# Reordering four small things in a TensorE-bound kernel: square, gate, weights' sums and a check line

## The chip, the cores and the metric

The kernel runs on one core of a Trainium2 chip. The metric is the device time of one execution in microseconds (us), the median of several runs. Every comparison below is between runs in the same state; all runs of this case were in the fast state, and every kernel named here gave a correct result.

## The reference

Two blocks follow one another. The first is a gated linear attention with a complex decay per step (4 batches, 8 heads, 768 steps, head size 48); the second multiplies its output (3072 x 384) by a weight matrix, applies h * cos(h), and multiplies by a second weight matrix.

```python
# attention, for every batch and head, step t
scale = min(mag, 0.999) / (mag + 1e-6)          # mag = |a_re + i a_im|
new_re = ar * S_re - ai * S_im                  # ar, ai: a_re, a_im times scale
new_im = ar * S_im + ai * S_re
S_re, S_im = new_re + outer(k[t], v[t]), new_im
y[t] = q[t] @ S_re
# ... x = y laid out as (3072, 384) ...
h = x @ w_in                                    # (3072, 2048)
g = h * np.cos(h)
out = g @ w_out                                 # (3072, 384)
```

## The kernel before

The kernel works through 24 chunks of 128 steps in 12 groups of two. In each group ("n" below) TensorE computes one group's scores and states, the "hp" phase (x times w_in, eight tiles of 128 x 512 in PSUM, 12 matmul records each), and the products with w_out. The scheduler weaves the steps of neighbouring groups together; each engine then runs its own list in a fixed order, and `behind(a, b)` only says "a comes after b in that order", without any new semaphore.

These are the parts that the change touches. The eight hp tiles share three PSUM buffers (two of tag "m", one "acc"):

```python
def mm1(g, jp):                       # one hp tile and its gate
    ps = pm.tile([C, 2, G * C], F32, tag="acc" if third else "m", name="hp",
                 bufs=1 if third else 2)
    # ... 2 x 3 matmuls into ps ...
    special(out=gate, in_=ps, func=AF.Sin, scale=1.0 / in_scale, bias=half_pi_b)   # ScalarE: cos
    vector.tensor_tensor(out=gate, in0=ps, in1=gate, op=ALU.mult)                  # VectorE: h * cos
    scalar.activation(out=junk, in_=ps, func=AF.Square, scale=1.0 / in_scale,      # ScalarE: only for
                         accum_out=wide[:, ds(g * (NJ // 2) + jp, 1)])             #   the check
```

```python
def f_transpose(g, i, n, name):       # kT and qT of the next group; VectorE, then DMAs
    # ...
    vector.transpose(out=tr, in_=X[g][name[0] + "s"][:, ds(i * H, n * H)].rearrange(...))
    nc.sync.dma_start(out=moved..., in_=tr)
    # kT: four dma_starts; qT: one
    nc.sync.dma_start(out=X[g][name][:, :, ds(i * H, n * H)], in_=moved.rearrange("q c x j -> c q x j"))

# differences of quarters of w_out (the code's "t1, t2, t4"), for a product scheme with fewer matmuls
for t, a, b in (t1, b12, b11), (t2, b22, t1), (t4, b21, t2):
    yield lambda t=t, a=a, b=b, j=j: vector.tensor_tensor(
        out=t[:, ds(j, 2)], in0=a[:, ds(j, 2)], in1=b[:, ds(j, 2)], op=ALU.subtract)
```

At the end a "check line" of 224 single words is written to memory in two pieces (`low`, `even`), read back as one row, and reduced to one flag (`bad`). The flag says whether the fast path was allowed for these inputs.

```python
nc.sync.dma_start(out=line_d[0:D2], in_=low.rearrange("p o -> (p o)"))       # 96 single words
nc.sync.dma_start(out=line_d[D2:D2 + C], in_=even.rearrange("p o -> (p o)")) # 128 single words
nc.sync.dma_start(out=line, in_=line_d.unsqueeze(0))
nc.vector.tensor_reduce(out=bad[:, 0:1], in_=line, axis=AX.X, op=ALU.min)
```

Of the kernel before, what the change touches and what calls it, by code (L numbers as in the profile page):

```python
# [18 lines left out]
ALU = mybir.AluOpType  # L19
AX = mybir.AxisListType  # L20
# [466 lines left out]
def fast_path(ctx, tc, q, k, v, a_re, a_im, moe_w_in, moe_w_out, out, least, odd, wide):  # L487
# [6 lines left out]
    nc = tc.nc  # L494
    B, H, S, D = q.shape
    DM, DF = moe_w_in.shape
    C = 128
    NCH = S // C
    G = 2
    N = B * NCH  # L500
    NG = N // G
    D2 = 2 * D
    HH = H // 2
# [3 lines left out]
    NJ = DF // C  # L507
# [34 lines left out]
    X = [dict() for _ in range(NG)]  # L542
    Y = [dict() for _ in range(N)]
# [32 lines left out]
    causal = constant(causal_np * np.float32(0.25), "causal")  # L576
# [63 lines left out]
    in_scale = 2.0 if moe_w_in.dtype != F32 else 1.0  # L640
    out_scale = 2.0 if moe_w_out.dtype != F32 else 1.0

    tail = {}

    def chain(ins, engine="scalar"):
# [5 lines left out]
    def behind(ins, other):  # L651
        tc.add_manual_dep(ins.ins, other.ins.name, mybir.DependencyInfo(
            mybir.DependencyClass.NoSync, mybir.DependencyReason.DATA))
# [5 lines left out]
    class Ordered:  # L659
# [7 lines left out]
        def __getattr__(self, op):  # L667
            def call(**kw):
                ins = getattr(self.engine, op)(**kw)  # L669
                if Ordered.by_hand:  # L670
                    chain(ins, self.name)
                elif self.name in Ordered.mark:
                    behind(ins, Ordered.mark[self.name])
            return call

    vector, scalar = Ordered(nc.vector, "vector"), Ordered(nc.scalar, "scalar")
# [176 lines left out]
    def f_transpose(g, i, n, name):  # L853


        if i == 0:
            X[g][name] = ft.tile([D2, G * H, Q4, 32] if name == "kT" else [D2, Q4, G * H, 32], F32,
                                 tag=name, name=name, bufs=1)
        tr = ft.tile([C, NB, n * H, 32], F32, tag="tr", name="tr")
        vector.transpose(out=tr, in_=X[g][name[0] + "s"][:, ds(i * H, n * H)].rearrange(  # L860
            "p x a d -> p x (a d)").rearrange("p x (r b) -> p b x r", b=NB))
        moved = rows_d.tile([Q4, D2, n * H, 32], F32, tag="moved", name="moved", bufs=3)
        nc.sync.dma_start(out=moved.rearrange("q (r b) x j -> (q r) b x j", b=NB), in_=tr)
        if name == "kT":
            for q4 in range(Q4):
                nc.sync.dma_start(out=X[g][name][:, ds(i * H, n * H), q4], in_=moved[q4])
        else:
            nc.sync.dma_start(out=X[g][name][:, :, ds(i * H, n * H)],
                              in_=moved.rearrange("q c x j -> c q x j"))
# [18 lines left out]
    def f_scores(n, hh):  # L888
        y = Y[n]
        if hh == 0:  # L890
            y["atm"] = ft.tile([C, H, C], F32, tag="atm", name="atm")
        ps = pa.tile([C, HH, C], F32, tag="a", name="sc")
        for h in range(HH):
            head = hh * HH + h
            matmul(ps[:, h], lhsT=X[n // G]["kT"][:, n % G * H + head],
                   rhs=queries(n, head), start=True, stop=True)
        vector.tensor_tensor(out=y["atm"][:, ts(hh, HH)], in0=ps,
                                in1=causal.unsqueeze(1).to_broadcast([C, HH, C]), op=ALU.mult)

    def f_out(n):  # L900
        y, (g, i) = Y[n], divmod(n, G)
# [58 lines left out]
    def f_xt(g):  # L960

        moved = rows_d.tile([HH, 2, D, G * C], F32, tag="x", name="x")
        for side in range(2):
            nc.sync.dma_start(
                out=moved[:, side].rearrange("p d t -> d p t"),
                in_=X[g]["yT"][ds(side * 64, D)].rearrange("d p g t -> d p (g t)"))
        xt = X[g]["xT"] = msb.tile([C, ND, G, C], F32, tag="xT", name="xT")
        nc.sync.dma_start(
            out=xt.rearrange("p c g t -> p c (g t)"),
            in_=moved.rearrange("p s d t -> (p s d) t").rearrange("(c r) t -> r c t", r=C))  # L970

    def mm1(g, jp):
        x = X[g]
        third = len(x.setdefault("gate", {})) % 3 == 2
        ps = pm.tile([C, 2, G * C], F32, tag="acc" if third else "m", name="hp",
                     bufs=1 if third else 2)
        for ji in range(2):
            for dc in range(ND):
                matmul(ps[:, ji], lhsT=w_in[:, jp, dc, ts(ji, C)],
                       rhs=x["xT"][:, dc].rearrange("p g t -> p (g t)"),  # L980
                       start=(dc == 0), stop=(dc == ND - 1))
        gate = msb.tile([C, 2, G * C], F32, tag="gate", name="gate", bufs=8)
        junk = msb.tile([C, 2, G * C], BF16, tag="junk", name="junk", bufs=1)
        special(out=gate, in_=ps, func=AF.Sin, scale=1.0 / in_scale, bias=half_pi_b)
        vector.tensor_tensor(out=gate, in0=ps, in1=gate, op=ALU.mult)
        scalar.activation(out=junk, in_=ps, func=AF.Square, scale=1.0 / in_scale,
                             accum_out=wide[:, ds(g * (NJ // 2) + jp, 1)])
        x["gate"][jp] = gate

    def mm2(g, i, j0, nj):  # L990
# [20 lines left out]
    def quarters():  # L1011

        for name in "s1", "s2", "a22":
            right[name] = stage["pool"].tile([C, HJ, E2], F32, name="t_" + name)
        t1, t2, t4 = (right[name] for name in ("s1", "s2", "a22"))
        for j in range(0, HJ, 2):
            for t, a, b in (t1, b12, b11), (t2, b22, t1), (t4, b21, t2):
                yield lambda t=t, a=a, b=b, j=j: vector.tensor_tensor(
                    out=t[:, ds(j, 2)], in0=a[:, ds(j, 2)], in1=b[:, ds(j, 2)], op=ALU.subtract)

    def last_quarter():

# [25 lines left out]
    def seventh(g, p, part):  # L1048


        x, name = X[g], SEVEN[p]
        if p == 0 and part == 0:
            x["sum"] = pm.tile([C, E2], F32, tag="acc", name="sum", bufs=1)
            x["ot"] = [msb.tile([C, DM], F32, tag="ot", name="ot") for _ in range(G)]

        alone = g == NG - 1 and p == 6
        summed = p in (0, 3, 5, 6) and not alone
        if not summed and part == 0:
            x["op"] = pm.tile([C, E2], F32, tag="m", name="op", bufs=2)
        ps = x["sum"] if summed else x["op"]  # L1060
        for j in range(part * HJ // 2, (part + 1) * HJ // 2):
            matmul(ps, lhsT=left(g, name, j), rhs=right[name][:, j],
                   start=(j == 0 and (p == 0 or not summed)),
                   stop=(j == HJ - 1), skip_group_check=summed)
        if part == 0:
            return
        c11, c12, c21, c22 = (x["ot"][i][:, ts(half, E2)] for i in range(2) for half in range(2))
        if p in (0, 2, 5) or p == 6 and not alone:
            scalar.mul(out={0: c11, 2: c21, 5: c22, 6: c12}[p], in_=ps, mul=scale)
        if g == NG - 1 and p == 5:  # L1070
            scalar.mul(out=c12, in_=ps, mul=scale)
        if p in (1, 3, 4, 5) or alone:
            part_ = {1: c11, 3: c21, 4: c21, 5: c22, 6: c12}[p]
            vector.scalar_tensor_tensor(out=part_, in0=x["op"] if p == 5 else ps, scalar=scale,
                                        in1=part_, op0=ALU.mult, op1=ALU.add)
        row = g * G * C
        if g == NG - 1 and p == 1:
            nc.sync.dma_start(out=out[ds(row, C), 0:E2], in_=c11)
        elif p == 5:
            nc.sync.dma_start(out=out[ds(row + C, C), :], in_=x["ot"][1])  # L1080
        elif p == 6:
            nc.sync.dma_start(out=out[ds(row, C), ds(alone * E2, DM - alone * E2)],
                              in_=c12 if alone else x["ot"][0])
# [144 lines left out]
              (mixes(n, 0, 2), 0.9, 1.0), (guarded(n - 1, per) if n > 3 else [], 0.1, 0.9))  # L1228
    weave((mixes(NG - 1, 2, 4), 0.0, 0.1), (products(NG - 1, 0, 7), 0.0, 1.0))
    assert not guards  # L1230
@with_exitstack
def kernel(ctx, tc, q, k, v, a_re, a_im, moe_w_in, moe_w_out, out):

# [7 lines left out]
    NG, NJ = q.shape[0] * q.shape[2] // C // 2, moe_w_out.shape[0] // C  # L1241
    odd = keep.tile([C, moe_w_in.shape[0] // C * 4 + NJ + NG + 1], F32, name="odd")
    wide = keep.tile([C, NG * NJ // 2], F32, name="wide")
    fast_path(tc, q, k, v, a_re, a_im, moe_w_in, moe_w_out, out, least, odd, wide)
    low = keep.tile([D2, 1], F32, name="low")
    nc.vector.tensor_reduce(out=low, in_=least, axis=AX.X, op=ALU.min)
    even = keep.tile([C, 1], F32, name="even")
# [6 lines left out]
    scratch = ctx.enter_context(tc.tile_pool(name="scratch", bufs=1,  # L1254
                                             space=bass.MemoryType.DRAM))
    line_d = scratch.tile([D2 + C], F32, name="line_d")
    nc.sync.dma_start(out=line_d[0:D2], in_=low.rearrange("p o -> (p o)"))
    nc.sync.dma_start(out=line_d[D2:D2 + C], in_=even.rearrange("p o -> (p o)"))
    line = keep.tile([1, D2 + C], F32, name="line")
    nc.sync.dma_start(out=line, in_=line_d.unsqueeze(0))  # L1260
    bad = keep.tile([1, 2], F32, name="bad")
    nc.vector.tensor_reduce(out=bad[:, 0:1], in_=line, axis=AX.X, op=ALU.min)
    flag = keep.tile([1, 1], I32, name="flag")
    nc.vector.tensor_scalar(out=flag, in0=bad[:, 0:1], scalar1=0.5, scalar2=None, op0=ALU.is_lt)
    taken = nc.values_load(flag[0:1, 0:1], min_val=0, max_val=1,
# [33 lines left out]
```

## Time and profile before

| | kernel before |
|---|---|
| time, median of 3 runs (range) | 703.81 us (701.42 to 705.78) |
| span of the profiled run | 700.8 us |
| mean granted clock of TensorE | 0.981 |
| TensorE, VectorE, ScalarE busy | 94%, 69%, 55% |
| largest waits of TensorE that the change aims at | hp for the square 10.9 us in 9; hp for xT 2.6; phs for VectorE's tan 2.5; sum for ot 1.1 |
| length of an hp phase, with the wait / without | 22.13 us / 20.88 us |

TensorE is the bound, so the time can only be found in its gaps. In the list of waits a line reads: engine and tile that waited, what released it, total us, number of waits, the longest. In a timeline a line reads: start us, duration, engine, source line, operation, output from inputs, shapes, number of instructions in the stretch, and in brackets the idle time before it with what ended that. Tile names repeat: "junk" is the square's output, "gate" with "hp" among its inputs is VectorE's product, "tr" a transposition. The lines themselves are shown in the prediction.

### The profile page before, as it was taken

To read this page: it belongs to the slowest core of one execution; us is meant where nothing else is said; L and a number is where in the kernel's file an instruction comes from. 1 tells how busy PE (TensorE), PEld (TensorE's weight loads), DVE (VectorE), ACT (ScalarE), POOL (GpSimd) and SP (SyncE) were. 2 spreads that over 40 slices of the span, in tenths; PEclk is the share of its full clock that TensorE was granted. 3 is DMA by queue.
4 is the path that set the end of the run, shared out by engine and by line. 5 is a ranking of instruction groups with operands and counts; after the bars stand their busy time and mean duration, and the time that the engine had idled before them with its cause. 6 is when DMAs were issued, how large, how long until landed. Compare 5 with 4: busy or idle time off the path is not lost.

```text
span 700.8 us, 10680 instructions
## 1 busy us (share of the span) xinstructions
PE 659.7 (94%) x4060; PEld 579.7 (83%) x4060; DVE 480.9 (69%) x782; ACT 386.8 (55%) x710; POOL 26.1 (4%) x45
## 2 busy tenths in 40 slices
PE   5788898999999999999999999999999999899995
PEld 5686676886799899899899899899899899799894
DVE  4889899546767777776777777776777768752241
ACT  5867775374374376376376376376376376342330
POOL 1012100000000000000000000000000000000000
PEclk9978999999999999999999999999999999999999
DMA  9778707805636547656746747647746644453000
GB/s 256 154 226 253 189 21 144 207 1 124 169 68 124 168 116 162 171 119 151 189 113 137 204 112 154 180 118 160 182 112 156 183 114 73 131 135 91 23 1 29
DMA packets 232953, 94.96 MB, mean 136 GB/s; under 512 B 208814, under 2 KB 221361, under 8 KB 232892
## 3 DMA queue, kind: packets, MB, share of 16 engines
q1 hardware_dynamic: 226396, 68.68, 43.8%
q0 software_dynamic: 5632, 25.17, 10.7%
q8 instruction: 34, 0.56, 0.3%
q10 hardware_dynamic: 864, 0.33, 0.2%
q14 instruction: 27, 0.22, 0.1%
HBM read 69.35 MB, written 24.81 MB: 134 GB/s over the span
## 4 chain that ended last, share of the span: by engine, by line
PE 66%; DVE 16%; DMA 7%; ACT 7%; issue 2%; SPq 0%; POOL 0%; DVEq 0%; POOLq 0%
PE hp L679 24%; PE op L679 14%; PE sum L679 9%; PE sc L679 5%; DVE tr L669 5%; PE yp L679 5%; PE sp L679 3%; DVE qs L669 2%; PE phs L679 2%; DMA raw<-in_moe_w_out_dram 2%; PE lgs L679 2%; DVE w_out L669 2%; DVE ks L669 1%; ACT lg L698 1%; DMA xT<-x 1%
## 5 line engine op out<-in xcount | busy, mean ns | idle before, releaser
L679 PE MATMUL hp<-xT,w_in 128*128 128x256 f32 x1152 | 257.8, 384 | 14.1 <-ACT junk L669 10.9
L679 PEld LDWEIGHTS hp<-xT,w_in 128*128 128x128 f32 x1152 | 220.6, 192 | 49.7 <-ACT junk L669 14.5
L669 DVE TENSOR_TENSOR gate<-hp,gate 128x512 f32<-128x512 f32 x96 | 65.9, 686 | 88.7 <-ACT gate L698 87.8
L669 ACT ACTIVATE junk<-hp 128x512 bf16<-128x512 f32 x96 | 57.2, 596 | 94.1 <-DVE gate L669 94.1
L679 PE MATMUL op<-w_out,gate 128*128 128x192 f32 (+1 forms) x448 | 103.0, 379 | 0.6 <-DVE w_out L669 0.6
L679 PEld LDWEIGHTS op<-w_out,gate 128*128 128x128 f32 x448 | 76.5, 192 | 21.3 <-issue 3.2
L698 ACT ACTIVATE gate<-hp,half_pi_b 128x512 f32<-128x512 f32 x96 | 65.4, 684 | 44.6 <-PE hp L679 44.6
L679 PE MATMUL sum<-t_s,s 128*128 128x192 f32 x320 | 55.4, 326 | 1.1 <-DVE ot L669 1.1
L679 PEld LDWEIGHTS sum<-t_s,s 128*128 128x128 f32 x320 | 52.5, 190 | 1.4 <-DVE ot L669 1.4
L679 PEld LDWEIGHTS sc<-qT,kT 96*128 96x128 f32 x384 | 47.9, 192 | 2.7 <-ACT qT L669 1.2
L679 PE MATMUL sc<-qT,kT 96*128 96x128 f32 x384 | 49.2, 275 | 0.9 <-ACT qT L669 0.9
L669 ACT ACTIVATE ot<-sum 128x192 f32<-128x192 f32 x30 | 9.5, 320 | 59.7 <-PE sum L679 59.7
L669 DVE SCALAR_TENSOR_TENSOR ot<-op,ot 128x192 f32<-128x192 f32 x31 | 11.0, 356 | 39.9 <-ACT ot L669 26.3
L669 DVE TENSOR_TENSOR atm<-sc,causal 128x512 f32<-128x512 f32 x48 | 32.8, 684 | 6.0 <-PE sc L679 6.0
L694 ACT ACT_TABLE_LOAD x26 | 33.4, 1283 | 4.0 <-issue 3.6
L679 PE MATMUL yp<-atm,v 128*48 128x128 f32 x352 | 33.6, 277 | 0.6 <-DVE atm L669 0.6
L679 PEld LDWEIGHTS sp<-v,ks 128*96 128x96 f32 x320 | 29.7, 165 | 1.8 <-issue 1.0
L679 PE MATMUL yp<-qT,state 96*48 96x128 f32 x304 | 29.6, 272 | 0.0
L679 PE MATMUL sp<-v,ks 128*96 128x48 f32 x320 | 29.6, 245 | 0.0
L679 PE MATMUL sum<-w_out,gate 128*128 128x192 f32 x160 | 29.6, 329 | 0.0
L679 PE MATMUL op<-t_a,gate 128*128 128x192 f32 x160 | 29.0, 332 | 0.0
L669 ACT COPY yT<-yp 48x512 f32<-48x512 f32 x44 | 25.4, 577 | 6.5 <-PE yp L679 5.8
(123 smaller groups left out, 935.9 us busy)
## 6 DMA issues: line engine op xcount, KB each, us to landing
moved<-tr SPq DMA_DIRECT2D x20, 768.0 KB
raw<-in_moe_w_in_dram POOLq DMA_DIRECT2D x16, 768.0 KB, 6.1
raw<-in_moe_w_out_dram POOLq DMA_DIRECT2D x16, 768.0 KB, 5.0
kT<-moved SPq DMA_DIRECT2D x40, 192.0 KB
qT<-moved SPq DMA_DIRECT2D x10, 768.0 KB
k<-in_k_dram SPq DMA_DIRECT2D x24, 192.0 KB
q<-in_q_dram SPq DMA_DIRECT2D x24, 192.0 KB
v<-in_v_dram SPq DMA_DIRECT2D x24, 192.0 KB
```

The source lines that it names most:

```text
L669: ins = getattr(self.engine, op)(**kw)
L679: chain(nc.tensor.matmul(out, **kw), "tensor")
L694: chain(nc.scalar.preload_act_table_set(table))
L698: chain(nc.scalar.activation(func=func, **kw))
```

## The change

There are four parts. (1) In the hp phase ScalarE's square of a tile comes before VectorE's product, and VectorE runs the first tile's product between the two transpositions of the next group rather than behind both. (2) The weights' sums move from the crowded start of VectorE's list to a place behind the masks of the third group's scores. (3) The small transfer `low` goes behind the last transfer of xT. (4) The reduction `bad` goes behind the last output's addition. No matmul is added or removed. The diff, cut to its core (the omitted lines only hand instruction objects around):

```diff
@@ f_transpose
-        vector.transpose(out=tr, ...)
+        turn = vector.transpose(out=tr, ...)
+        if name == "qT" and "gated" in X[g - 1]:
+            behind(turn, X[g - 1]["gated"])
@@ f_scores
-        vector.tensor_tensor(out=y["atm"][:, ts(hh, HH)], in0=ps, ...)
+        y["masked"] = vector.tensor_tensor(out=y["atm"][:, ts(hh, HH)], in0=ps, ...)
@@ mm1
-        vector.tensor_tensor(out=gate, in0=ps, in1=gate, op=ALU.mult)
         scalar.activation(out=junk, in_=ps, func=AF.Square, ...)
+        gated = vector.tensor_tensor(out=gate, in0=ps, in1=gate, op=ALU.mult)
+        x.setdefault("gated", gated)
@@ the weights' sums
-                yield lambda t=t, a=a, b=b, j=j: vector.tensor_tensor(
-                    out=t[:, ds(j, 2)], in0=a[:, ds(j, 2)], in1=b[:, ds(j, 2)], op=ALU.subtract)
+                yield lambda t=t, a=a, b=b, j=j: behind(vector.tensor_tensor(
+                    out=t[:, ds(j, 2)], in0=a[:, ds(j, 2)], in1=b[:, ds(j, 2)],
+                    op=ALU.subtract), Y[PLAIN * G]["masked"])
@@ the check line
-    nc.sync.dma_start(out=line_d[0:D2], in_=low.rearrange("p o -> (p o)"))
+    behind(nc.sync.dma_start(out=line_d[0:D2], in_=low.rearrange("p o -> (p o)")), late["x"])
...
-    nc.vector.tensor_reduce(out=bad[:, 0:1], in_=line, axis=AX.X, op=ALU.min)
+    behind(nc.vector.tensor_reduce(out=bad[:, 0:1], in_=line, axis=AX.X, op=ALU.min), late["out"])
```

## The prediction

> **What bounds the kernel now.** I read the page first (busy time per engine), then the waits of TensorE, then the timeline of one steady group, the last groups and the end, and last the busy time by stretch for the start. The work is done in 12 groups of two chunks; each has a phase of eight "hp" tiles (x times the first weight matrix; 96 matmul records a group, 12 a tile), which ScalarE and VectorE turn into gates.
>
> The page's first part, busy us, share of the span and instructions; then TensorE's waits: total us, times, longest:
>
> ```profile
> PE 659.7 (94%) x4060; PEld 579.7 (83%) x4060; DVE 480.9 (69%) x782; ACT 386.8 (55%) x710; POOL 26.1 (4%) x45
> ...
> PE hp L679 <- ACT junk L669: 10.9, 9, 3.1
> PE phs L679 <- ACT tan L698: 4.0, 2, 2.7
> ...
> PE hp L679 <- DMA xT<-x: 2.6, 1, 2.6
> PE phs L679 <- DVE tan L669: 2.5, 2, 2.0
> PE sum L679 <- DVE ot L669: 1.1, 1, 1.1
> ```
>
> TensorE is the bound: 660 of 701 us. The change takes no matmul away and, as the comparison of the two programs' orders shows, leaves the order of TensorE and GpSimd exactly as it was. So all it can win is TensorE's idle time (some 41 us, of which the start and the end cannot be had) and time at a reduced clock. The largest named wait is the first: hp waits for the ScalarE square ("junk"). The timeline of a steady group (start us, duration, engine):
>
> ```profile
> 232.43 7.93 PE L679 MATMUL hp<-xT,w_in 128*128 128x256 f32 x36
> ...
> 235.22 0.69 ACT L698 ACTIVATE gate<-hp,half_pi_b 128x512 f32<-128x512 f32 x1 [2.24 <-PE hp L679]
> ...
> 235.53 2.24 DVE L669 STREAM_TRANSPOSE tr<-ks 128x1536 f32<-128x1536 f32 x1
> ...
> 237.75 2.24 DVE L669 STREAM_TRANSPOSE tr<-qs 128x1536 f32<-128x1536 f32 x1
> ...
> 239.92 0.64 DVE L669 TENSOR_TENSOR gate<-hp,gate 128x512 f32<-128x512 f32 x1
> 240.60 0.60 ACT L669 ACTIVATE junk<-hp 128x512 bf16<-128x512 f32 x1 [4.69 <-DVE gate L669]
> ...
> 241.34 3.94 PE L679 MATMUL hp<-xT,w_in 128*128 128x256 f32 x17 [0.98 <-ACT junk L669]
> ```
>
> There are three PSUM buffers for hp. Three tiles are 36 matmuls, so the fourth (due at about 240.0) needs the first one back. The first tile was ready at 235; its sine ran at once; but the VectorE product stood behind two transpositions of 2.24 us, and the square behind the product. ScalarE sat idle 4.69 us for it.
>
> [...] sine, product and square of a tile never overlap, and the square waited for the product 79 times (94.1 us in ScalarE's waits). [...]
>
> **Part 1: square before product, first gate between the transpositions.** The sum of a tile's own three steps stays (0.69 + 0.60, or 0.73 with the accumulator's read, + 0.69, about 2.1 us). But the square now follows the sine at once, 235.9 to 236.6, and the product needs only VectorE: behind the first transposition, 237.8 to 238.5. That gives the buffer back at 238.5 in place of 241.2, 1.5 us before the fourth tile is due. The second transposition then runs 238.5 to 240.7, the second product to 241.4; the fifth tile is due a tile (2.57 us) after the fourth, at 242.5. So the wait should vanish. Its worth is not 0.98 (ends of matmuls are modelled) but the length of the whole phase: 232.43 to 241.34 + 13.22 (the chain's remaining 60) = 254.56, so 22.13 us, against 20.88 us for the 96 of the last group, which has no wait. The same sums give 1.16 us in the third group and 1.25 in each of seven more: **9.9 us**.
>
> **Part 2: the start, where the weights are converted.** Busy us by stretch (TensorE, weight loads, VectorE, ScalarE, GpSimd), granted clock, DMA:
>
> ```profile
> 40.00:60.00 20.00, 16.67 (x73) 14.20 (x71) 16.56 (x24) 16.49 (x22) 2.41 (x3) 0.74 0.72 227
> 60.00:80.00 20.00, 15.42 (x49) 11.21 (x50) 16.33 (x23) 15.83 (x28) 3.83 (x5) 0.83 0.90 246
> 80.00:100.00 20.00, 19.37 (x91) 13.86 (x90) 19.96 (x31) 15.66 (x27) 0.72 (x1) 1.00 0.24 60
> 100.00:120.00 20.00, 17.99 (x149) 14.04 (x148) 19.18 (x32) 11.60 (x20) 0.00 (x0) 0.94 0.51 107
> ```
>
> The wait of 3.1 us (58.8 to 61.9) goes, since the new ScalarE order is sine, square, sine, square ahead of the conversions' casts; the exponentials and the phase matmul (waited 2.7 us) come some 4 us earlier. But from 80 to 117 VectorE is full and TensorE waits for it (0.6 us for the last w_out, 2.0 us for tan at 116.9). VectorE's work is fixed, so what counts is VectorE: the idle time it recovers between 60 and 80 (3.7 us, of which I give 2, as the products still wait for squares), and the weights' sums that leave this stretch (before 116.9: six sums of 0.55 us, 3.2 us on the clock). That would be about 5; TensorE itself can gain only 0.6 + 2.0 plus what the earlier conversions bring, and the last w_out fetches, freed by VectorE, come later in the new order. I take **4.5 us**, the softest term. The sums land at 150 to 170, where VectorE is about 55% busy (10.62 and 11.24 of 20 us); they put at most 1.1 us before the log that TensorE needs at 160.0, which was ready at 156.96. No cost.
>
> **Part 3: the check line's first half behind the last xT.** The eleventh group's hp starts late:
>
> ```profile
> 593.73 0.31 SPq L1257 DMA_DIRECT2D line_d<-low  x1
> ...
> 594.15 0.38 SPq L968 DMA_DIRECT2D xT<-x  x1
> ...
> 603.65 8.69 PE L679 MATMUL hp<-xT,w_in 128*128 128x256 f32 x39 [2.63 <-DMA xT<-x]
> ```
>
> From issue to use is 9.5 us here; in an earlier group 6.9 us (382.9 to 389.9) were enough without a wait. In the timeline, a transfer of this kind ("even", 0.5 KB of single words) took 6.4 us from its issue at 677.7 until the next one could be issued at 684.1. "low" now goes behind xT: I take 2.3 of the 2.6 us.
>
> **Part 4: the check line's reduction last.** Now it blocks VectorE for its DMA:
>
> ```profile
> 687.24 0.37 DVE L1262 TENSOR_REDUCE bad<-line 1x1 f32<-1x224 f32 x1 [7.50 <-DMA line<-line_d]
> ...
> 687.75 0.36 DVE L669 SCALAR_TENSOR_TENSOR ot<-sum,ot 128x192 f32<-128x192 f32 x1
> ...
> 688.17 2.87 PE L679 MATMUL sum<-t_s,s 128*128 128x192 f32 x16 [1.08 <-DVE ot L669]
> ```
>
> The "ot" sum had its operand at about 684.3; without the block TensorE loses nothing: **1.2 us**. What comes after the last matmul (693.6 to 700.8) I leave: the last output still goes out after it.
>
> Sum: 9.9 + 4.5 + 2.3 + 1.2 = 17.9. From it I take 1.6 for new small waits: 703.8 - 17.9 + 1.6 = **687.5 us**, 2.3% less.
>
> **Rivals.** (a) A transfer takes the wait's place. The second transposition ends 0.7 us later and TensorE reaches the next scores 1.25 us earlier. In one group qT's transfer is issued at 245.87, DMA traffic ends at about 251, the scores start at 254.4: 3 us of room, 1 left. The tightest is 561.70, 567, 569.55: 2.4 us, some 0.4 left. If it runs out, up to 1 us a group returns, and the time is about 694. (b) The start gives nothing, because VectorE stays full until the last w_out and its new order puts conversions behind the gates, so the log of the next group slips: about 692. Against it: 3.2 us of sums do leave. (c) The start gives more: without the stall of 3.1 us the clock stays up and TensorE's 60 to 80 shrinks as well; about 683. (d) VectorE becomes the bound in the hp phase: no, a pair of tiles costs it two products and four sums (2 x 0.69 + 4 x 0.42 = 3.1 us) in 5.1 us.
>
> **Range and chances.** Parts 1 and 4 are read from gaps that the new order removes by construction, 11.1 us together, with qT as the risk; they alone give 692.7, 1.6% less. Whether 2% (689.7) is passed hangs on parts 2 and 3. All good gives 682, only part 1 with some loss 694. Faster by over 2%: 0.66; within: 0.33; slower: 0.01, as nothing is added.
>
> **What would show it.** Part 1: in the waits no "hp <- junk", nor a new "hp <- gate"; every steady hp phase 20.9 us; one product between the transpositions. Part 2: hp's fourth tile of the first group starts near 59, clock above 0.8 in 40 to 80, the phase matmul at 116.9 comes at about 112. Part 3: no wait for xT. Part 4: no idle TensorE between the last products, "bad" without a wait. I am wrong if scores wait for kT or qT, or if VectorE reaches the end of the w_out conversions no earlier than 98 us.

## The result, and the profile after

| | before | after |
|---|---|---|
| time, median of 4 runs each, same rounds (range) | 703.16 us (701.42 to 705.78) | 684.19 us (683.15 to 686.43) |
| ratio, 95% interval | | 0.9731 (0.9691 to 0.9772): faster |
| span of the profiled run, mean clock | 700.8 us, 0.981 | 681.9 us, 0.987 |

A ratio here is the mean time of one kernel's fast runs over the mean time of the other's in the same rounds, so it is not quite the ratio of the two medians. Where a gain in us is given from a ratio below, it is (1 - ratio) times the median of the kernel before in that set of runs.

The page of the changed kernel, first part (busy us, share of the span, instructions):

```profile
PE 653.7 (96%) x4060; PEld 577.7 (85%) x4060; DVE 480.3 (70%) x782; ACT 382.5 (56%) x710; POOL 27.3 (4%) x45
```

The instruction counts of TensorE, VectorE and ScalarE are those of before: only order has changed. The waits of TensorE in the changed kernel:

```profile
PE phs L683 <- ACT tan L702: 4.2, 2, 2.8
...
PE op L683 <- DVE w_out L672: 2.3, 3, 1.1
PE phs L683 <- DVE tan L672: 2.1, 4, 0.8
PE sc L683 <- DMA qT<-moved: 1.3, 2, 0.9
```

Three of the four entries that the change aimed at, hp for junk, hp for the xT transfer and sum for VectorE's ot, are no longer in the list. The fourth, phs for VectorE's tan, fell only from 2.5 to 2.1 us in all; its longest piece fell from 2.0 to 0.8. Two things are new or larger: TensorE waits 2.3 us for converted weights (0.6 before), and 1.3 us for the qT transfer, which was no wait before. The timeline of a steady hp phase after the change, one group after the one the prediction shows:

```profile
277.80 13.54 PE L683 MATMUL hp<-xT,w_in 128*128 128x256 f32 x62
...
280.90 2.25 DVE L672 STREAM_TRANSPOSE tr<-ks 128x1536 f32<-128x1536 f32 x1
281.18 0.59 ACT L672 ACTIVATE junk<-hp 128x512 bf16<-128x512 f32 x1
...
283.12 0.69 DVE L672 TENSOR_TENSOR gate<-hp,gate 128x512 f32<-128x512 f32 x1
...
283.72 2.25 DVE L672 STREAM_TRANSPOSE tr<-qs 128x1536 f32<-128x1536 f32 x1
```

The square runs beside the first transposition, the product comes between the two, and the row of hp matmuls runs on past the 36th without a break (62 in one stretch, ended by other work woven in). Taking the first and last hp matmul of every group, groups 2 to 12 all last 20.88 us.

The busy time by stretch in the start (columns as in the prediction), two of the four stretches:

```profile
60.00:80.00 20.00, 16.84 (x70) 12.92 (x69) 19.35 (x29) 17.16 (x30) 3.62 (x5) 1.00 0.86 227
...
100.00:120.00 20.00, 18.77 (x129) 13.15 (x126) 17.63 (x26) 10.19 (x17) 0.00 (x0) 1.00 0.70 140
```

VectorE now works 19.35 of 20 us between 60 and 80 (16.33 before), with a granted clock of 1.00 (0.83 before); between 100 and 120 it has room again. The second group's hp phase starts at 121.2 against 127.1.

The eleventh group's transfer of xT (the last but one), its hp phase, and the small transfer, which now goes behind the twelfth group's xT, the last:

```profile
579.63 0.38 SPq L974 DMA_DIRECT2D xT<-x  x1
...
587.41 2.97 PE L683 MATMUL hp<-xT,w_in 128*128 128x256 f32 x13
...
628.26 0.48 SPq L1272 DMA_DIRECT2D line_d<-low  x1
```

From issue to use is 7.8 us instead of 9.5, with no wait in brackets. The end:

```profile
669.82 2.76 PE L683 MATMUL sum<-t_s,s 128*128 128x192 f32 x16
...
672.42 2.76 PE L683 MATMUL op<-w_out,s 128*128 128x192 f32 x16
...
673.26 0.36 DVE L1278 TENSOR_REDUCE bad<-line 1x1 f32<-1x224 f32 x1
```

The reduction no longer waits, and the products follow one another without idle time.

Where the 18.9 us of span went, from the starts of the hp phases in the two traces (the first starts 0.2 us apart): group 2 starts 5.9 us earlier (127.1 against 121.2), group 10 13.4 us earlier (547.6 against 534.2), group 11, where the xT wait went, 16.2 us (603.6 against 587.4), group 12 17.1 us, and the end is 18.9 us earlier. Between the starts of groups 2 and 10 seven phases became 8.7 us shorter in all, but the start of group 10 gained only 7.5 of that; the new waits for qT lie in this stretch.

### The profile page after: what moved, and what is told of

The parts are those of the page before. It is cut to its first block, busy times and chain, and to the rows that moved or that the text cites. A ratio compares the mean times of both kernels' runs of the same rounds, so it can differ in the third digit from the quotient of the medians.

```text
span 681.9 us, 10685 instructions
## 1 busy us (share of the span) xinstructions
PE 653.7 (96%) x4060; PEld 577.7 (85%) x4060; DVE 480.3 (70%) x782; ACT 382.5 (56%) x710; POOL 27.3 (4%) x45
## 3 DMA queue, kind: packets, MB, share of 16 engines
q1 hardware_dynamic: 226396, 68.68, 44.6%
q0 software_dynamic: 5632, 25.17, 11.0%
## 4 chain that ended last, share of the span: by engine, by line
PE 84%; DMA 5%; DVE 5%; ACT 4%; issue 1%; DVEq 0%; ACTq 0%
PE hp L683 31%; PE op L683 17%; PE sum L683 15%; PE sc L683 6%; PE yp L683 5%; PE sp L683 3%; PE lgs L683 2%; DMA raw<-in_moe_w_out_dram 2%; PE phs L683 2%; DMA qT<-moved 2%; DVE w_in L672 1%; ACT raw L672 1%; DVE w_out L672 1%; PE yr L683 1%; DMA im<-in_a_im_dram 1%
## 5 line engine op out<-in xcount | busy, mean ns | idle before, releaser
L683 PE MATMUL hp<-xT,w_in 128*128 128x256 f32 x1152 | 253.6, 382 | 0.6 <-ACT xT L672 0.6
L683 PE MATMUL op<-w_out,gate 128*128 128x192 f32 (+1 forms) x448 | 101.6, 375 | 2.3 <-DVE w_out L672 2.3
L672 ACT CAST tan<-phs 128x384 int32<-128x384 f32 x24 | 11.5, 479 | 30.8 <-PE phs L683 30.6
```

The source lines that it names most:

```text
L672: ins = getattr(self.engine, op)(**kw)
L683: chain(nc.tensor.matmul(out, **kw), "tensor")
```

## The experiments

Runs that stand in one set ran on the same chip beside the same runs of the kernel before. Each kernel was timed in five rounds.

### First set: one part alone, on the kernel before

The kernel before had a median of 703.63 us here (27 runs).

**e1_swap_only**: only the order of square and product.

```diff
-        vector.tensor_tensor(out=gate, in0=ps, in1=gate, op=ALU.mult)
         scalar.activation(out=junk, in_=ps, func=AF.Square, ...)
+        vector.tensor_tensor(out=gate, in0=ps, in1=gate, op=ALU.mult)
```

> Edit: the kernel before, with only the square put ahead of the product. Theory A (the release of the first PSUM tile is the limit, and it still stands behind both transpositions): product of the first tile at 239.98 to 240.65 in the old clock, the fourth tile due at 240.0, so a wait of some 0.7 us remains in 8 groups, now 'hp <- gate' in place of 'hp <- junk'; steady hp phase about 21.5 us (before 22.13, after 20.88), 0.55 x 8 = 4.5 us gained. In the start the wait of 3.1 us at 58.8 vanishes and the second group's hp phase starts 2 to 3 us earlier than 127.1. Time 7 us less than before. Rival B (the swap is the whole cure, the order of the transpositions is decoration): steady phase 20.9 us, time 13 us or more less.

Measured: 694.24 us, ratio 0.9871 (0.985 to 0.9892), 9.1 us less. The timeline of a steady phase in e1_swap_only:

```profile
284.04 2.25 DVE L669 STREAM_TRANSPOSE tr<-ks 128x1536 f32<-128x1536 f32 x1
...
286.26 2.27 DVE L669 STREAM_TRANSPOSE tr<-qs 128x1536 f32<-128x1536 f32 x1
...
288.44 1.26 DVE L669 TENSOR_TENSOR gate<-hp,gate 128x512 f32<-128x512 f32 x2
...
289.15 2.21 PE L680 MATMUL hp<-xT,w_in 128*128 128x256 f32 x9 [0.28 <-DVE gate L669]
```

The square is out of the way, but the product still stands behind both transpositions and the buffer comes back at about 289.1, just too late: a short wait for "gate" takes the place of the one for "junk" (2.6 us in 9 over the kernel). The phase lasts 21.43 us: 0.70 less than before, 0.55 more than without a wait. Over the eight phases that is 5.6 of the 9.9 us. The rest comes from the start, where the second group's hp begins at 123.5 instead of 127.1, 3.6 us earlier where 2 to 3 were expected.

**e2_turn_only**: only the product between the transpositions; the square stays behind the product.

```diff
-        vector.transpose(out=tr, ...)
+        turn = vector.transpose(out=tr, ...)
+        if name == "qT" and "gated" in X[g - 1]:
+            behind(turn, X[g - 1]["gated"])
...
-        vector.tensor_tensor(out=gate, in0=ps, in1=gate, op=ALU.mult)
+        gated = vector.tensor_tensor(out=gate, in0=ps, in1=gate, op=ALU.mult)
+        x.setdefault("gated", gated)
```

> Edit: the kernel before, with only the first product put between the two transpositions (the square stays behind the product). Theory A: product 237.8 to 238.5, square to 239.2, its accumulator's read to 239.4, and the tile is due at 240.0: no wait, though the old order of square and product stays. Steady hp phase 20.9 us, 9.9 us gained, start unchanged (wait of 3.1 us at 58.8 stays, second hp phase at 127). Time 10 us less than before. Rival B (swap needed): a wait of 0.5 us or more stays in each group, less than 6 us gained. Rival C (qT's transfer is late): scores wait for qT in two or three groups, 2 us of the 10 lost.

Measured: 693.54 us, ratio 0.9869 (0.9839 to 0.9899), 9.2 us less. The timeline of a steady phase in e2_turn_only:

```profile
284.13 2.25 DVE L669 STREAM_TRANSPOSE tr<-ks 128x1536 f32<-128x1536 f32 x1
...
286.34 0.70 DVE L669 TENSOR_TENSOR gate<-hp,gate 128x512 f32<-128x512 f32 x1
...
286.94 2.27 DVE L669 STREAM_TRANSPOSE tr<-qs 128x1536 f32<-128x1536 f32 x1
287.07 0.60 ACT L669 ACTIVATE junk<-hp 128x512 bf16<-128x512 f32 x1 [2.56 <-DVE gate L669]
```

The square still waits 2.56 us for the product, and it does not matter: it ends at 287.7. The phase began at 281.04, and 36 matmuls take some 7.8 us of it, so the fourth tile is due only at about 288.9. All steady phases last 20.88 us. In the steady groups the turn alone is enough; the swap adds nothing there. The stall of 3.1 us at the start stays, as no instruction moved there. The second hp phase came at 124.9 all the same, not at 127 as expected; the paragraph behind e8 says why.

**e3_sums_only**: only the weights' sums behind the third group's masks.

```diff
-                yield lambda t=t, a=a, b=b, j=j: vector.tensor_tensor(
-                    out=t[:, ds(j, 2)], in0=a[:, ds(j, 2)], in1=b[:, ds(j, 2)], op=ALU.subtract)
+                yield lambda t=t, a=a, b=b, j=j: behind(vector.tensor_tensor(
+                    out=t[:, ds(j, 2)], in0=a[:, ds(j, 2)], in1=b[:, ds(j, 2)],
+                    op=ALU.subtract), Y[PLAIN * G]["masked"])
```

> Edit: the kernel before, with only the twelve sums of the second weight matrix put behind the third group's masks. Theory A (VectorE bounds 80 to 117 us): the phase matmul that waited at 116.9 comes 2.0 to 3.2 us earlier without a wait, and as TensorE does not idle there its clock stays up (the 24 op matmuls that took 9.53 us take about 8.0), so the second hp phase starts 3 to 4.5 us earlier than 127.1; the 3.1 us wait at 58.8 stays; steady phases as before. Time 3 to 4 us less. Rival D (the sums were beside other work and cost nothing): within 1 us of before.

Measured: 701.94 us, ratio 0.9976 (0.9967 to 0.9985), 1.7 us less. The expectation was too high. The mechanism is there: the wait of phs for VectorE's tan fell from 2.5 us (longest 2.0) to 1.3 (longest 0.8). The second hp phase did start 3.9 us earlier in this profile (123.2), as expected, but 1.6 us of that is the faster run of 24 matmuls that e2 shows without moving the sums (granted clock 1.00 from 100 to 140 in both, 0.94 and 0.97 in before), and the profiled run was the fastest of the 22 (700.31 us).

**e4_line_only**: both check-line moves, parts 3 and 4.

```diff
-    nc.sync.dma_start(out=line_d[0:D2], in_=low.rearrange("p o -> (p o)"))
+    behind(nc.sync.dma_start(out=line_d[0:D2], in_=low.rearrange("p o -> (p o)")), late["x"])
...
-    nc.vector.tensor_reduce(out=bad[:, 0:1], in_=line, axis=AX.X, op=ALU.min)
+    behind(nc.vector.tensor_reduce(out=bad[:, 0:1], in_=line, axis=AX.X, op=ALU.min), late["out"])
```

> Edit: the kernel before, with only the two moves of the check line (low behind the last xT, the reduction behind the last output's sum). Theory A: no wait of 2.6 us for xT in the eleventh group, no 1.1 us wait of sum for ot at 688: 3.8 us less. Rival E (xT is late for another reason, such as the traffic before it): the wait for xT stays at 2 us or more and only 1.2 us is gained.

Measured: 697.5 us, ratio 0.9914 (0.9894 to 0.9934), 6.1 us less, against 3.8 expected. The waits for xT and for ot are gone and nothing else moved. The surplus had to be taken apart; e11 and e12 below do that.

### Second set: the changed kernel with one part taken back

The kernel before had a median of 703.4 us here (9 runs).

**e5_no_swap**: the changed kernel with the product before the square again.

```diff
+        gated = vector.tensor_tensor(out=gate, in0=ps, in1=gate, op=ALU.mult)
         scalar.activation(out=junk, in_=ps, func=AF.Square, ...)
-        gated = vector.tensor_tensor(out=gate, in0=ps, in1=gate, op=ALU.mult)
```

> Edit: the changed kernel with the square put back behind the product; all else of the change stays. Theory A (after the runs so far: the move of the first product cures the steady groups, the square's move works in the start): steady hp phases stay 20.9 us, as with the first product's move alone; the wait of 3.1 us at 58.8 comes back and the second group's hp phase starts at 123 to 124 (after: 121.2; the sums' move alone: 123.2). Time 2 to 3 us over the changed kernel, ratio to before about 0.977. Rival B (both moves are needed in the steady groups when the sums and the check line are moved too): steady phases over 21.2 us, 5 us over the changed kernel.

Measured: 686.32 us, ratio 0.9754 (0.9734 to 0.9773). Steady phases 20.88 us; the 3.1 us stall of the start is back, and only there.

**e6_no_turn**: the changed kernel without the turn.

```diff
-        if name == "qT" and "gated" in X[g - 1]:
-            behind(turn, X[g - 1]["gated"])
```

> Edit: the changed kernel without the one dependency that holds the second transposition behind the first product. Theory A: steady phases 21.43 us as with the square's move alone (0.55 us lost in 8 groups, 4.4 us), start as after (121.2), and the scores' waits for qT (2 us in three groups after) go away, as TensorE gets there later and the transposition earlier: net 2.5 us over the changed kernel, ratio about 0.977. Rival: no waits for qT were due to the move, so 4.4 us over it (0.979 to 0.98) and waits for qT still there.

Measured: 685.71 us, ratio 0.9754 (0.9738 to 0.9769). Steady phases 21.43 us again, with the wait of hp for gate (2.8 us in 9), and no wait for qT at all.

**e7_no_sums**: the changed kernel with the sums where they were.

```diff
-                yield lambda t=t, a=a, b=b, j=j: behind(vector.tensor_tensor(
-                    out=t[:, ds(j, 2)], in0=a[:, ds(j, 2)], in1=b[:, ds(j, 2)],
-                    op=ALU.subtract), Y[PLAIN * G]["masked"])
+                yield lambda t=t, a=a, b=b, j=j: vector.tensor_tensor(
+                    out=t[:, ds(j, 2)], in0=a[:, ds(j, 2)], in1=b[:, ds(j, 2)], op=ALU.subtract)
```

> Edit: the changed kernel with the twelve sums of the second weight matrix back where they were. Theory A: the start is that of the square's move alone: second hp phase at 123.5 (after 121.2), phase matmul again waits about 2 us for tan; everything later as after: 2.3 us over the changed kernel, ratio about 0.976. Rival (sums and square each free the same idle time): second hp phase at 121.5, no loss.

Measured: 686.27 us, ratio 0.9773 (0.9753 to 0.9793). The wait of phs for tan is 2.6 us with its 2.1 us piece back. This run's profile also waits 2.2 us for qT, which the sums have no visible hand in; see the third set.

**e8_qt_gpsimd**: the changed kernel with the qT transfer issued from GpSimd's queue.

```diff
-            nc.sync.dma_start(out=X[g][name][:, :, ds(i * H, n * H)],
+            nc.gpsimd.dma_start(out=X[g][name][:, :, ds(i * H, n * H)],
```

> Edit: the changed kernel with the transfer qT issued from GpSimd's queue in place of SyncE's, where it stands behind four issues of kT. Theory A (the wait for qT comes from the issue, which can stall on SyncE's queue: 2.8 us in one group): no wait of scores for qT, 1 to 2 us less than the changed kernel, ratio about 0.971. Rival (the 128-byte pieces of kT and qT fill the DMA engines from end to end, so the last one lands when it did): same time within 1 us and the waits stay; GpSimd's issue could even make it later.

Measured: 682.05 us, ratio 0.9699 (0.9684 to 0.9714), no wait for qT. TensorE waits once for kT instead, 0.7 us. It looked like a version that beats both kernels, but the changed kernel itself was not in this set, so it had to be run beside it. For the same reason the times of e5, e6 and e7 alone don't show what each part is worth: their intervals overlap that of the changed kernel's first runs (0.9691 to 0.9772). What carries the argument there is the phases and waits in their traces.

The start can be read from all fourteen traces (those of the next sets too) as the distance between the first and the second hp phase. It is 78.4, 78.6, 76.5, 78.3 and 78.3 us where neither swap nor sums moved (before, e4, e2, e11, e12); 75.0 and 75.0 with the swap alone (e1, e7); 75.2 and 76.1 with the sums alone (e3, e5); 72.7, 73.9, 74.0, 72.5 and 72.6 with both (after, e6, e8, e9, e10). The means are 78.0, 75.0, 75.7 and 73.1: 3.0 us for the swap, 2.3 us for the sums, 4.9 us for both. The scatter is a microsecond or two: the same 24 "op" matmuls after the same stall of 2.0 us took 9.53 us in the trace of before, at a granted clock of 0.94 and 0.97 in the two stretches that they lie in, and 7.90 us at 1.00 in e2, whose order up to there is the same. Under e12 the clock's records give the reason.

### Third set: qT on the same chip, and the small transfer alone

The kernel before had a median of 702.7 us here (19 runs).

**e9_after_again**: the changed kernel, unaltered.

> The changed kernel again, unaltered, so that it stands beside the next run on one chip. Expected from its earlier times: 683 to 686 us, ratio to before 0.971 to 0.976. Its profile should show waits of TensorE for the qT transfer of about 1 to 2 us in all, as in the first profile of it.

**e10_qt_again**: the kernel of e8 once more, beside it.

> The changed kernel with the qT transfer issued from GpSimd's queue, again, beside the run above on one chip. Theory (the waits for qT are true losses and the queue of SyncE is their cause): no wait for qT on TensorE, and 1 to 3 us less than the changed kernel beside it, 681 to 684 us. Rival (the earlier 682.1 us was the chip's scatter): no difference beyond 0.5 us.

Measured: e9 682.35 us, ratio 0.9717 (0.9684 to 0.975); e10 682.88 us, ratio 0.972 (0.9689 to 0.9752). The rival holds: no difference beyond the scatter. The traces show that the wait comes and goes with the same program. First the tightest group in the first profile of the changed kernel:

```profile
547.77 2.81 SPq L874 DMA_DIRECT2D qT<-moved  x1
...
556.04 1.13 PE L683 MATMUL sc<-qT,kT 96*128 96x128 f32 x8 [0.94 <-DMA qT<-moved]
```

and the same group in e9_after_again, the same kernel in another run:

```profile
547.24 0.99 SPq L874 DMA_DIRECT2D qT<-moved  x1
...
554.31 1.06 PE L683 MATMUL sc<-qT,kT 96*128 96x128 f32 x8
```

The issue took 2.81 us in one run and 0.99 in the other (the ten issues of qT took 0.92 to 2.81 us in the first trace, with a median of 1.23), and the wait is there in one and not in the other. Over the whole kernel the waits for qT were 1.3 us, 0.5 in e9 (1 to 2 were expected) and 2.2 in e7 with the transfer on SyncE's queue, but none in e5, where it is on that queue too; and none in e8 and e10 with it on GpSimd's. The room for qT has become so small that a late issue shows, but the timed runs put the cost at no more than the scatter. Why an issue is sometimes late is open. Of the traces with qT on SyncE's queue, the seven without the turn have no issue above 1.58 us, and four of the five with it have one of 1.90 to 2.81 (e9 has none).

**e11_low_gpsimd**: the kernel before, with only `low` on another queue. It was meant to separate "behind it on the same queue" from "beside it on the same DMA engines".

```diff
-    nc.sync.dma_start(out=line_d[0:D2], in_=low.rearrange("p o -> (p o)"))
+    nc.gpsimd.dma_start(out=line_d[0:D2], in_=low.rearrange("p o -> (p o)"))
```

> The kernel before, with one line altered: the single-word check-line transfer (low) is issued from GpSimd's queue, so that it isn't ahead of the last xT transfer on SyncE's queue; everything else stands. Theory (the transfer ahead on the same queue delays xT): the last xT lands 7.3 to 7.8 us after its issue, or is issued earlier, and the last phase's wait for xT (2.6 us before) goes; 700.5 to 702 us, 2 to 3 us under before. Rival (the small transfer delays xT through the shared DMA engines, whichever queue it takes): the wait stays at 2 us or more and the time within 1 us of before.

Measured: 699.03 us, ratio 0.9945 (0.9927 to 0.9962), 3.9 us less. The timeline around the last-but-one xT in e11_low_gpsimd:

```profile
593.56 0.38 SPq L968 DMA_DIRECT2D xT<-x  x1
593.61 0.54 POOL L1257 DMA_DIRECT2D line_d<-low  x1 [14.49 <-DVE low L1246]
...
600.45 2.75 PE L679 MATMUL hp<-xT,w_in 128*128 128x256 f32 x12
```

The two transfers are issued within 0.05 us of each other, and xT is used 6.9 us after its issue without a wait, against 9.5 us in before and 9.9 in e12. With `low` ahead on the same queue (before, e1, e2, e3, e12) the packets of this xT took 8.0 to 9.3 us from the first to the last in the DMA records; half of them were through within 1.6 us, but single ones lasted up to 6.6 to 7.6 us. In e11, in e4 and in the changed kernel they took 1.5 to 1.7 us. So `low` ahead of xT is what delays it. Whether the place on the queue is the cause, or the 96 single words, this run does not separate, because the edit changed both: by the pages' DMA counts SyncE's queue lost 112 packets (226396 before, 226284 in e11) and GpSimd's gained only 32 (5632, 5664). The words no longer went one by one. That single words would disturb xT from any queue is a rival that no run here tests.

### Last run: the reduction alone

**e12_reduction_last**: the kernel before with only part 4. The kernel before had a median of 702.46 us here (27 runs).

```diff
-    nc.vector.tensor_reduce(out=bad[:, 0:1], in_=line, axis=AX.X, op=ALU.min)
+    behind(nc.vector.tensor_reduce(out=bad[:, 0:1], in_=line, axis=AX.X, op=ALU.min), late["out"])
```

> The kernel before with only the check line's reduction (bad) moved behind the last output's addition; the small transfer (low) stays where it was. It measures part 4 alone. The prediction's own figure, the gap of TensorE at the end: 1.2 us less, ratio 0.9983. Theory after the first runs (both check-line moves together gave 6.1 us and the small transfer alone 3.7 by its ratio, and the changed kernel ends 1.8 us sooner after the last hp phase): 1.8 to 2.4 us less, ratio 0.9966 to 0.9974. Both expect no wait of sum for the ot sum, and that the wait of about 2.6 us for the last xT stays.

Measured: 700.07 us, ratio 0.9964 (0.9952 to 0.9976), 2.5 us less. The wait for ot is gone; the one for xT stays, as it should. Its profiled span, 701.0 us, shows none of the gain, and looking for the reason brought out what the wait for xT really costs. The timeline of that hp phase in e12_reduction_last, then the busy time in two stretches of 3.41 us around its start (columns as in the prediction):

```profile
603.69 22.67 PE L681 MATMUL hp<-xT,w_in 128*128 128x256 f32 x96 [3.07 <-DMA xT<-x]
```

```profile
601.13:604.54 3.41, 0.85 (x4) 0.77 (x5) 3.41 (x4) 0.00 (x0) 0.00 (x0) 1.00 0.39 120
604.54:607.95 3.41, 3.41 (x10) 2.69 (x9) 1.16 (x1) 0.00 (x0) 0.00 (x0) 0.50 0.42 173
```

and the time around it in e11_low_gpsimd, where xT came in time:

```profile
600.00:610.00 10.00, 10.00 (x49) 8.86 (x48) 9.93 (x11) 3.86 (x9) 0.00 (x0) 1.00 0.32 128
```

Behind the wait of 3.07 us the granted clock is 0.50 for 3.41 us, and the phase lasts 22.67 us where 20.88 is usual: the wait costs 1.8 us more than its own length. That fits an estimate: half of 3.41 us is 1.7. Five traces have this wait:

| trace | wait for xT, us | hp phase behind it, us | both, over 20.88 |
|---|---|---|---|
| before | 2.63 | 20.99 | 2.7 |
| e3_sums_only | 2.50 | 22.67 | 4.3 |
| e12_reduction_last | 3.07 | 22.67 | 4.9 |
| e2_turn_only | 3.10 | 22.61 | 4.8 |
| e1_swap_only | 3.86 | 23.77 | 6.8 |

In the trace of before, on which the prediction was built, the clock happened to stay at 1.00. In the other four it did not. The mean of the last column is 4.7 us.

The clock's records in the traces say what decides. In all fourteen the granted clock is 1.00 or 0.50, and it changes only at whole steps of 3.41 us. Each trace was cut into these steps, from its first record (at 7 to 10 us) to about 10 us before its end. There were 35 steps at full clock with 2.0 us or more of idle TensorE, and every one was followed by a step at 0.50. Of the steps with less idle time only one in each trace was; it ends between 42 and 46 us and has 0.3 to 1.0 us of idle time, and its cause is open. The wait of 2.63 us in before fell across two steps (598.90 to 602.31 and 602.31 to 605.72, with 1.30 and 1.34 us idle), that of 2.50 us in e3 into one (596.21 to 599.62). In the start, the step with the stall for tan had 2.01 us idle in before (half clock behind it, 24 matmuls in 9.53 us) and 1.85 in e2 (full clock, 7.90 us). So whether a wait of two or three microseconds costs clock depends on where it falls in these steps.

Parts 3 and 4 alone, 3.9 and 2.5 us, make 6.4 us, where both together (e4) gave 6.1: the surplus of e4 is settled.

## Why the prediction was right

The prediction said 687.5 us, in a range of 682 to 694; the measurements were 684.19 us and, repeated, 682.35 us. Direction and mechanism held; two terms of the sum were too small, the allowance was hardly needed, and one term was credited to the wrong edit. By its own steps:

- **Part 1, the square and the first gate: 9.9 us.** The size was right: eight phases fell to 20.88 us. What the prediction did not see is that it credited two edits with what one does. Its own timeline had the numbers. With the turn alone the product ends at 238.5, the square about 0.6 later at 239.1, still before the fourth tile is due at 240.0; with the swap alone the product ends at 240.6, 0.6 too late. e1 and e2 measured just that: 5.6 of the 9.9 us from the swap, all of it from the turn. So the single gains overlap: 9.1 (e1), 9.2 (e2), 1.7 (e3), 3.9 (e11) and 2.5 (e12) sum to 26.4 us, 5.6 of them counted twice, which leaves 20.8, against 18.9 (first runs, by the ratio) and 19.9 (e9) for the whole.
- **Part 2, the start: 4.5 us.** The two traces compared first show 5.9 us, but 1.6 us of it is the slower run of 24 matmuls in the trace of before. Over fourteen traces the start gained 4.9 us; alone the swap gives 3.0, which is its real use, and the sums 2.3. Rival (c), the clock, is part of it in some runs: behind the stall of 2.0 to 2.1 us those 24 matmuls were slow in two of seven traces (before and e4), and behind the stall of 0.8 us that the sums leave in none of seven. The prediction's marks came true in part: the fourth hp tile follows without a break, the clock is 1.00 between 60 and 80, and the last conversion of w_out ends at 94.1 instead of 98.0; but between 40 and 60 the clock stayed at 0.74. The phase matmul came at 112.75, not at 116.94. The mark of the clock rested on a misreading: the prediction took 0.74 as the work of the wait of 3.1 us, but the half clock of that stretch lay at 42.5 to 52.8, before the wait at 58.8, and lies at 43.1 to 53.3 after the change. And the 1.00 between 60 and 80 is luck in part: e6 and e8, whose swap and sums are the changed kernel's, had a step of 3.41 us at half clock there, and their start took 73.9 and 74.0 us instead of 72.5 to 72.7.
- **Part 3, the small transfer: 2.3 us.** Mis-sized. That `low` ahead of xT causes the wait is shown by e4 and e11; that its place on the queue does it was the author's assumption and is not shown, as e11 changed the packets too. And the term was read as the length of a wait in one trace, and alone the move measured 3.9 us (2.7 to 5.1). What the step left out is the clock: in four of five traces the wait was followed by a slower hp phase, so that it cost 4.3 to 6.8 us there and 2.7 in the trace of before. The prediction counted on a reduced clock in the start alone. By the clock's records under e12 the effect depends on where in the steps of 3.41 us a wait falls: 2.50 us within one step cost clock and 2.63 us across two did not.
- **Part 4, the reduction last: 1.2 us.** Too small as well: 2.5 us (1.7 to 3.4) alone. The last hp phase ends 26.7 us before the end of the span in the kernel before, 24.9 in the changed one, 24.6 in e4. The gap of TensorE that the prediction counted is there; the half microsecond and more on top lies after the last sixteen products start (9.91 us to the end before, 9.45 after, 9.12 in e4), which the prediction left out on purpose. Over the fourteen traces it is 9.8 us on average in the five that leave the reduction where it was and 9.3 in the nine that move it, so it goes with the move; but the two overlap (e1, which does not move it, has 9.26; e10, which does, 9.65), and how the move would do it is not shown.
- **The allowance, 1.6 us, and rival (a).** The transfer of qT did begin to be waited for, as the prediction feared for its tightest group, but with 0.5 to 2.2 us in all, not up to 1 us a group. Timed side by side, its removal gave nothing.
- **Rivals (b) and (d).** The start gave what was predicted, so (b) fell. VectorE is not the bound in the hp phase, as all phases last 20.88 us; so (d) fell.

What stays open: why single issues of a qT transfer take 2.8 us instead of 1.0, why the clock halves for 7 to 10 us from between 42 and 46 us in all fourteen traces, how moving the reduction shortens the end of the span by half a microsecond, and whether `low` delays xT by its place on the queue or by its single words. The version with qT on GpSimd's queue is not shown to beat the changed kernel.

## What to carry to other kernels

When the bounding engine waits for a buffer, write down for each user of that buffer when it can run and when the buffer is due; the smallest move that meets the due time is enough, and a second edit for the same gap is worth nothing there. Test edits singly: gains of edits that serve one gap do not add, and an edit made for one place (the swap) can earn its keep in another (the start). Price a wait of two or three microseconds on TensorE over several traces, with the length of the phase behind it: one trace may have missed the clock's share, which here hung on whether 2.0 us of idle time fell into one step of 3.41 us. A bookkeeping transfer of a few hundred bytes belongs behind the large transfers of its queue (or on another queue, which gave 3.9 us here but was tested only together with a change of its packets), and a bookkeeping reduction behind the last useful work of its engine (2.5 us here).
